# Scores tiled by 64-query blocks of both heads, with four score banks, two transfers of P and an earlier scale of V

## The chip, the cores and the metric

The kernel runs on one core of a Trainium2 chip. The metric is the device time of one execution in microseconds (us). The time before is a median of 3 runs; the profile is of one further execution.

## What is computed

Eight sequences of 576 positions go through a causal attention of 8 heads of width 64 with a window of 128 positions and a bias that falls linearly with the distance, and then through a gated MLP with a spatial mixing:

```python
scores = q @ k.T / 8 + slope[head] * -|i - j|      # only 0 <= i - j < 128, else -1e9
attn = softmax(scores);  x = attn @ v              # the heads side by side: [576, 512]
h = relu(x @ w_in);  u, v = h[:, :512], h[:, 512:]
v_n = (v - mean) / sqrt(var + 1e-6)
out = (u * (w_spatial @ v_n + b_spatial)) @ w_out
```

All of it is to float32 precision, so the kernel splits many operands into a high and a low part and multiplies three times.

## The kernel before

Sequence 0 is done by a special path (`raw_tile`), together with the splitting of the weights. Sequences 1 to 7 are done in four pairs of heads each, 28 pairs in all. What is told here is the work of one pair.

`scores` loads q and k (`qkraw`, three buffers) and v (`vraw`, three buffers). `products` multiplies q by k in blocks of 64 queries: block i has as keys the blocks i-2 to i, so 64 columns (i = 0), 128 (i = 1) or 192. One matmul is a 64x64 tile of the TensorE array: head j of the pair lies in rows 64j to 64j+63 (the array's row half), and the output goes to partitions 0 to 63 or 64 to 127 (its column half). A tile of scores before is two blocks of ONE head, even block in the lower partitions and odd block in the upper ones: 4 tiles for each head, of 128, 192, 192 and 192 columns, and a ninth of 256 columns, in which both heads' last block stand. The tiles of head 0 lie in the PSUM banks s0 and s1, those of head 1 in s2 and s3. The ninth lies in the right half of bank x0 (`plan.kept["y"]`), the bank whose left half takes the output of attention times V.

For each tile VectorE adds the bias table and takes the minimum of the negated scores (L594), ScalarE does the exponential with its sum (L599). Then, for one group of tiles at a time (j = 0: four tiles, j = 1: five), VectorE forms the reciprocals of the sums (L618, L622), ScalarE writes P's high part in fp16 to `pq` (L628), VectorE its low part (L633), and DMA transposes bring `pq` into `pt` with the keys on the partitions (L642). There is one transfer for each group and partition half: four a pair, each of 64 rows.

`attention` finds a power of two to scale V by: ScalarE takes the sum of absolute values (L654), VectorE spreads it (L661), a small DMA transpose brings it onto all partitions (L665), VectorE takes the maximum and forms the scale in five small instructions (L670 to L674), and V is split into `vh` and `vl` (L678 or L681, L685). TensorE multiplies P by V in 42 matmuls (L701) into the banks x0 and x1, and ScalarE and VectorE write the two parts of x (`xt`, L712 and L716).

`gated` runs the MLP of a sequence: V units (L768, L790) with a layer norm, u units (L820), spatial units (L841), output units (L867). The outputs are copied to `o` (L314, two buffers before) and sent off by L877.

A planner (`Plan`) sets the order of all of it. Each piece of work is added with its engine, a duration that the planner assumes and a due time; the planner plays this through and at each moment takes, of what is ready on an engine, the piece that is due first. The order that comes out is fixed at build time, and on the chip each engine keeps to it: a piece that waits holds up all that stands behind it on its engine. SyncE issues all transfers, in one order too. An attention is added only after the scores of the next pair (`AHEAD = 1`).

Of the kernel before, what the change touches and what calls it, by code (L numbers as in the profile page):

```python
# [55 lines left out]
class Plan:  # L56
# [8 lines left out]
    def __init__(self):  # L65
        self.ops, self.tags, self.kept = [], {}, {}
# [9 lines left out]
    def add(self, engine, weight, due, fn, reads=(), writes=()):  # L76
        self.either([(engine, weight, fn)], due, reads, writes)
# [22 lines left out]
    def order(self):  # L100
# [12 lines left out]
        while events or any(ready.values()):  # L113
# [8 lines left out]
            for e, heap in ready.items():  # L122
                if heap and free[e] <= now:
# [28 lines left out]
def attn_gmlp_kernel(ctx, tc, qk, v, w_in, w_spT, b_sp, w_out, outT):  # L152
# [17 lines left out]
    T0, TN = 2 * D, 3 * W  # L170
    HEAD = T0 + TN
    QSPLIT = 2 * P

# [23 lines left out]
    plan.kept["y"] = [plan.kept["x"][0][:, 2 * P:]]  # L197

# [23 lines left out]
    tabl = fixed([P, NP, 2 * P], BF16, "tabl")  # L222
# [6 lines left out]
    NT = 2 * (NQ - 1) + 1  # L229
    prob = fixed([P, 2 * HEAD + 2 * P], F32, "prob")  # L230
    PLANE = [7 * P, 9 * P]
    BASE = [0, 2 * PLANE[0] + D]
    BLOCK = [0, 14]
    PQ = BASE[1] + 2 * PLANE[1] + D
    pq = fixed([P, PQ], F16, "pq")
    stat = [fixed([P, 4, NT], F32, f"stat{i}") for i in range(2)]

# [58 lines left out]
    def tables():  # L296
        plan.add("POOL", 700, 60000, lambda: nc.gpsimd.memset(tabl(), MASKED), (), [(tabl, 0), (tabl, 1)])
        heads = [(told, h) for h in range(H)]
        for i in range(2):
            rows, cs = slice(i * D, (i + 1) * D), slice(i * D, i * D + W)  # L300

            def f(rows=rows, cs=cs):
                nc.sync.dma_start(tabs()[rows], told()[rows, :, cs])
            plan.add("SP", 800, 60000, f, heads, [(tabs, i)])

            def f(rows=rows, cs=cs, i=i):
                src = told()[rows].rearrange("p (a b) n -> p a b n", b=2)
                nc.sync.dma_start(tabl()[rows, :, (1 - i) * D:(1 - i) * D + W], src[:, :, i, cs])
            plan.add("SP", 800, 60000, f, heads, [(tabl, i)])
# [233 lines left out]
    def clear():  # L543
        plan.add("POOL", 2500, 0, lambda: nc.gpsimd.memset(pq(), 0.0), (), parts(pq, 0, PQ, 64))
# [6 lines left out]
    def pieces(p):  # L551
        out = []
        for j in range(2):
            for t in range(NQ - 1):
                n = T0 if t == 0 else W
                out.append((2 * j + (t == 3), (2 * W, 0, W, 0)[t], n, j * HEAD + (0 if t == 0 else T0 + (t - 1) * W),
                            BASE[j] + (0 if t == 0 else T0 + (t - 1) * 2 * P + D), PLANE[j], lambda h=2 * p + j, n=n: tabs()[:, h, W - n:]))
        out.append((4, 0, 2 * P, 2 * HEAD, BASE[1] + PLANE[0], PLANE[1], lambda: tabl()[:, p, :]))
        return out

    def products(p, due, st, raw, RAWS, first):
# [3 lines left out]
        flat = lambda k: sc[k]() if len(sc[k]().shape) == 2 else sc[k]().rearrange("p a b -> p (a b)")  # L565
        tiles = pieces(p)
        if first:
            def f():
                for j in range(2):
                    nc.vector.memset(flat(2 * j)[:D, 2 * W:2 * W + D], MASKED)  # L570
                nc.vector.memset(sc[4]()[:D, :D], MASKED)
                nc.vector.memset(sc[4]()[D:, W:], MASKED)
            plan.add("DVE", 400, due - 5500, f, (), [(x, 0) for x in sc])

        def f():
            def one(k, c0, j, half, i, back):
                a, z = max(0, (i - 2) * D), (i + 1) * D
                nc.tensor.matmul(flat(k)[half * D:(half + 1) * D, c0 + a - back:c0 + z - back], raw()[j * D:(j + 1) * D, 0, i * D:z],  # L578
                                 raw()[j * D:(j + 1) * D, 1, a:z], start=True, stop=True, skip_group_check=True)
            for j in range(2):  # L580
                one(4, (1 - j) * D, j, j, 2 * NQ - 2, (2 * NQ - 4) * D)
            for t in range(NQ - 1):
                for half in range(2):
                    for j in range(2):
                        i = 2 * t + half
                        one(tiles[j * (NQ - 1) + t][0], tiles[j * (NQ - 1) + t][1], j, half, i, (i - 2) * D + (D if t == 0 else 0))
        plan.add("PE", SWITCH + pe(*[4 * W] * NQ), due - 5000, f, RAWS, [(x, 0) for x in sc])
        for k, (bank, c0, n, pc, _, _, tab) in enumerate(tiles):
            pt = lambda pc=pc, n=n: prob()[:, pc:pc + n]
            t, j = (NQ - 1, 0) if k == NT - 1 else (k % (NQ - 1), k // (NQ - 1))  # L590
            d = due - 4500 + t * 700 + j * 200
# [369 lines left out]
```

## Time and profile before

| | us |
|---|---|
| median of 3 runs (lowest, highest) | 649.78 (649.24, 650.79) |
| the profiled execution, its own time | 649.93 |
| its span, first to last instruction | 648.2 |
| TensorE busy / idle in the span | 592.7 / 55.5 |
| VectorE busy | 517.1 |
| ScalarE busy | 379.8 |

The mean granted clock of TensorE is 0.983 of full speed. The 28 pairs are under way from about 75 us to 583 us of the span; ahead of that stand sequence 0 and the weights, after it the last two sequences' MLP. Busy time of TensorE is the time in which at least one matmul runs; the rest is idle, and the views of waits tell for each engine which instruction of another engine, or which transfer (DMA), ended an idle stretch.

### The profile page before, as it was taken

The numbers are of one execution on the slowest core, as the hardware profiler recorded it, in microseconds if no ns is written. First come the engines' busy times: TensorE is split into PE (matmuls) and PEld (weight loads), VectorE is DVE, ScalarE is ACT, GpSimd is POOL, SyncE is SP. The second block draws the span as 40 slices with busy tenths as digits, with TensorE's granted clock in tenths as the row PEclk, the third lists the DMA queues.
The fourth block names the chain that finished last, engine by engine and source line by source line (L and its number), as shares of the span: only waits on it lengthen the run. The fifth ranks groups of instructions, "written<-read, shape, count | busy, mean of one in ns | idle before, by whom it ended". The sixth has DMA issues, their size and how long they took to land. (4 is left out here: it accounts for less than half of the span.)

```text
span 648.2 us, 14898 instructions
## 1 busy us (share of the span) xinstructions
PE 592.7 (91%) x5392; PEld 520.3 (80%) x5392; DVE 517.1 (80%) x1913; ACT 379.8 (59%) x1200; POOL 33.2 (5%) x53
## 2 busy tenths in 40 slices
PE   4886898989899989998999989998999989899997
PEld 2444568888699879897899969897899968898997
DVE  7999989979968797887869788888968899943632
ACT  4677667767836575556646575555746586822211
POOL 2000020000100001000100001000100001000100
PEclk9997799999999999999999999999999999999999
DMA  8952217679646694378636674478647774531001
GB/s 259 335 147 78 73 43 130 154 137 192 134 78 136 133 198 76 91 162 156 119 77 123 153 189 72 87 162 161 123 87 140 138 143 70 91 80 37 2 18 56
DMA packets 147502, 78.41 MB, mean 121 GB/s; under 512 B 126818, under 2 KB 138082, under 8 KB 147428
## 3 DMA queue, kind: packets, MB, share of 16 engines
q1 hardware_dynamic: 147428, 77.46, 55.6%
q8 instruction: 42, 0.69, 0.5%
q14 instruction: 32, 0.26, 0.1%
HBM read 37.13 MB, written 9.44 MB: 72 GB/s over the span
## 5 line engine op out<-in xcount | busy, mean ns | idle before, releaser
L599 ACT ACTIVATE prob<-prob,stat 128x192 f32<-128x192 f32 (+2 forms) x252 | 109.7, 437 | 28.6 <-DVE stat L594 28.5
L841 PE MATMUL m<-wsp,vn 128*128 128x288 f32 x768 | 122.6, 298 | 3.5 <-DVE o L314 1.8
L820 PE MATMUL m<-xt,win 128*128 128x288 f32 x768 | 111.7, 298 | 6.0 <-ACT u L318 1.8
L628 ACT ACTIVATE pq<-prob,stat 128x192 f16<-128x192 f32 (+2 forms) x252 | 92.4, 439 | 37.9 <-issue 24.7
L841 PEld LDWEIGHTS m<-wsp,vn 128*128 128x128 f32 x768 | 107.5, 188 | 8.6 <-DVE o L314 3.4
L867 PE MATMUL m<-gs,wout 128*128 128x288 f32 x768 | 111.1, 299 | 2.2 <-DVE u L319 1.4
L820 PEld LDWEIGHTS m<-xt,win 128*128 128x128 f32 x768 | 103.8, 188 | 11.2 <-ACT u L318 3.8
L867 PEld LDWEIGHTS m<-gs,wout 128*128 128x128 f32 x768 | 103.8, 188 | 6.8 <-DVE u L319 1.7
L768 PE MATMUL m<-win,xt 128*128 128x512 f32 x384 | 94.3, 399 | 1.7 <-DVE vt L799 1.0
L633 DVE SCALAR_TENSOR_TENSOR pq<-prob,stat,pq 128x192 f16<-128x192 f32 (+2 forms) x252 | 90.8, 404 | 2.0 <-ACT pq L628 1.9
L768 PEld LDWEIGHTS m<-win,xt 128*128 128x128 f32 x384 | 72.2, 191 | 20.5 <-ACT pq L628 1.7
L849 DVE TENSOR_TENSOR u<-m,u 128x288 f32<-128x288 f32 x64 | 29.1, 454 | 45.5 <-PE m L841 45.2
L594 DVE CUSTOM_DVE_ANT_0 prob<-s,tabs 128x128 f32<-128x128 f32 (+1 forms) x224 | 62.9, 336 | 1.4 <-PE s L578 1.3
L738 POOL TENSOR_TENSOR st<-st,nhalf 128x1 f32<-128x1 f32 (+1 forms) x40 | 25.7, 643 | 557.2 <-DVE st L734 201.1
L578 PE MATMUL s<-qkraw 64*64 64x192 f32 (+2 forms) x896 | 50.5, 319 | 0.0
L599 ACT ACTIVATION_READ_ACCUMULATOR prob<-prob,stat 128x1 f32 x252 | 47.3, 188 | 0.0
L701 PE MATMUL x<-pt,vh 128*64 128x128 f16 (+2 forms) x784 | 43.8, 230 | 3.2 <-DMA pt<-pq 3.2
L318 ACT ACTIVATE u<-m 128x288 f32<-128x288 f32 x53 | 21.5, 405 | 40.5 <-PE m L820 40.5
L701 PEld LDWEIGHTS <-vh 128*64 128x64 f16 x784 | 35.0, 110 | 10.1 <-issue 5.5
L314 ACT COPY o<-m 128x288 f32<-128x288 f32 x28 | 11.2, 400 | 51.1 <-PE m L867 46.8
L578 PEld LDWEIGHTS s<-qkraw 64*64 64x64 f32 x896 | 39.2, 137 | 0.9
L701 PE MATMUL x<-pt,vl 128*64 128x256 f16 x392 | 35.7, 228 | 0.9 <-DVE vl L685 0.9
(139 smaller groups left out, 817.3 us busy)
## 6 DMA issues: line engine op xcount, KB each, us to landing
qkraw<-in_qk_dram SPq DMA_DIRECT2D x28, 576.0 KB, 4.5
out_dram<-o SPq DMA_DIRECT2D x64, 144.0 KB, 2.4
vraw<-in_v_dram SPq DMA_DIRECT2D x28, 320.0 KB, 3.8
vn<-in_w_in_dram SPq DMA_DIRECT2D x6, 512.0 KB, 7.9
wout<-in_w_out_dram SPq DMA_DIRECT2D x4, 512.0 KB, 7.9
pt<-pq SPq DMA_TRANSPOSE x112, 4.2
gs<-in_w_spT_dram SPq DMA_DIRECT2D x4, 288.0 KB, 5.0
xt<-in_w_in_dram SPq DMA_DIRECT2D x2, 512.0 KB, 6.6
```

The costliest lines, as they stand in the source:

```text
L578: nc.tensor.matmul(flat(k)[half * D:(half + 1) * D, c0 + a - back:c0 + z - back], raw()[j * D:(j + 1) * D, 0, i * D:z], raw()[j * D:(j + 1 ...
L594: nc.vector.tensor_tensor_reduce(pt(), flat(bank)[:, c0:c0 + n], tab(), -0.125, 3e38, ALU.add, ALU.min, st()[:, NM, k:k + 1])
L599: nc.scalar.activation(pt(), pt(), AF.Exp, bias=st()[:, NM, k:k + 1], scale=-1.0, accum_out=st()[:, SM, k:k + 1])
L628: nc.scalar.activation(pq()[:, qc:qc + n], prob()[:, pc:pc + n], AF.Copy, scale=st()[:, RC, k:k + 1])
L633: nc.vector.scalar_tensor_tensor(pq()[:, qc + plane:qc + plane + n], prob()[:, pc:pc + n], st()[:, RC, k:k + 1], pq()[:, qc:qc + n], ALU.m ...
L701: nc.tensor.matmul(xp()[j * D:(j + 1) * D, x0:x0 + w], l()[:, kt, j * D:(j + 1) * D], pts().rearrange("p a b -> p (a b)")[:, c:c + w], sta ...
L738: nc.gpsimd.tensor_tensor(st()[:m, 11:12], st()[:m, 10:11], nhalf()[:m], ALU.pow)
L768: nc.tensor.matmul(pt(), xt[c]()[:, X0[a] + t * P:X0[a] + (t + 1) * P], win()[:, c, w, DH:DF], start=(n == 0), stop=(n == 3 * NC_ - 1))
L820: nc.tensor.matmul(pt()[:, :HS], win()[:, c, w, d * P:(d + 1) * P], xt[c]()[:, X0[a] + hf * HS:X0[a] + (hf + 1) * HS], start=(n == 0), sto ...
L841: nc.tensor.matmul(pt()[:, :HS], l, r, start=(n == 0), stop=(n == len(ops) - 1))
L849: nc.vector.tensor_tensor(u(), pt()[:, :HS], u(), ALU.mult)
L867: nc.tensor.matmul(pt()[:, :HS], wout[d]()[:, w, e * P:(e + 1) * P], gs[d]()[:, a, :], start=(n == 0), stop=(n == 3 * ND - 1))
```

## The change

1. A tile of scores is one block of 64 queries of BOTH heads. Head 0 stands in the lower partitions and head 1 in the upper ones, in odd blocks the other way round. There are again nine tiles, of 64, 128 and seven times 192 columns. The bias table `tabs` follows that; the ninth tile's own table `tabl` goes, and with it the memsets of masked corners in PSUM.
2. Even blocks go to the banks s0 and s1, odd blocks to s2 and s3. No tile of scores lies in x0 any more.
3. The groups for reciprocals and transfers are the five even blocks and the four odd ones. P goes out in two transfers a pair, of 128 rows each, 18 and 14 blocks of 128 columns.
4. In P times V the columns of one matmul are picked in runs of 64 from the even and the odd part of `pt` (`queries`).
5. In the planner: the loads of q, k and v are due 4 us earlier, the scale of V 5 us earlier; a transfer of P is taken as 3 us and lands 1 us later, the small transfer of V's scale lands 1.5 us later (`lag`).
6. The output tile `o` has four buffers instead of two.

```diff
-    def add(self, engine, weight, due, fn, reads=(), writes=()):
+    def add(self, engine, weight, due, fn, reads=(), writes=(), lag=0):
+        self.late[len(self.ops)] = lag
...
+                    end += self.late.get(n, 0)
...
-    plan.kept["y"] = [plan.kept["x"][0][:, 2 * P:]]
...
-    PLANE = [7 * P, 9 * P]
-    BASE = [0, 2 * PLANE[0] + D]
+    BLOCKS = [*range(0, NB, 2), *range(1, NB, 2)]
+    EVENS = (NB + 1) // 2
+    WIDTH = [min(i + 1, 3) * D for i in BLOCKS]
+    PLANE = [2 * EVENS * P - P, 2 * (NB - EVENS) * P - P]
+    BASE = [0, 2 * PLANE[0]]
...
-    WINDOWS = (((0, (0, 256), 0), (1, (2 * P, 128), 128)),
-               ((1, (3 * P, 128), 0), (2, (4 * P, 256), 0), (3, (6 * P, 128), 128), (3, (0, None), 256), (4, (P, None), 256)))
+    WINDOWS = (((0, 4, 0, 0), (1, 2, 0, 128)),
+               ((1, 2, 1, 0), (2, 4, 0, 0), (3, 2, 0, 128), (3, 1, 1, 256), (4, 1, 0, 256)))
+    def places(k):
+        i = BLOCKS[k]
+        bank, c0 = ((0, 3 * P), (2, 3 * P), (0, 0), (2, 0), (0, W), (2, W), (1, 0), (3, 0), (1, W))[i]
+        odd = i % 2
+        return i, odd, bank, c0, sum(WIDTH[:k]), BASE[odd] + (0 if i < 2 else P + (i // 2 - 1) * 2 * P + odd * D), WIDTH[k]
+    def queries(pts, j, a, kt, n, s):
+        x = [BASE[o] + a * PLANE[o] + 2 * kt * P + s * P + (j ^ o) * D for o in range(2)]
+        flat = pts().rearrange("p a b -> p (a b)")
+        if n == 1:
+            return flat[:, x[0]:x[0] + D]
+        ap = flat[:, x[0]:x[0] + D]
+        steps = [[x[1] - x[0], 2], [1, D]]
+        return bass.AP(ap.tensor, ap.offset, [ap.ap[0], [P, 2], *steps] if n == 4 else [ap.ap[0], *steps])
...
-        sc = [plan.buf(ps, "s", 4, [P, 512], F32) for _ in range(4)] + [plan.buf(ps, "y", 1, [P, 2 * P], F32)]
+        sc = [plan.buf(ps, "s", 4, [P, 512], F32) for _ in range(4)]
...
+            order = sorted(range(NB), key=lambda k: (BLOCKS[k] // 2, BLOCKS[k]))
+            for k in order:
+                i, odd, bank, c0, _, _, n = places(k)
                 for j in range(2):
+                    rows = slice((j ^ odd) * D, ((j ^ odd) + 1) * D)
+                    nc.tensor.matmul(flat(bank)[rows, c0:c0 + n], raw()[j * D:(j + 1) * D, 0, i * D:(i + 1) * D],
+                                     raw()[j * D:(j + 1) * D, 1, (i + 1) * D - n:(i + 1) * D], start=True, stop=True, skip_group_check=True)
...
-            d = due - 4500 + t * 700 + j * 200
+            d = due - 4500 + k * 350
...
-        raw, vr = load(b, p, [due - 12000], [NQ])
+        raw, vr = load(b, p, [due - 16000], [NQ])
...
-            ks = range(NQ - 1) if j == 0 else range(NQ - 1, NT)
+            ks = range(EVENS) if j == 0 else range(EVENS, NB)
...
-            for half in range(2):
-                c0 = BASE[j] + (1 - half) * D
-                def f(j=j, half=half, nb=nb, c0=c0):
-                    rows = slice(half * D, (half + 1) * D)
-                    nc.sync.dma_start_transpose(out=pts()[:, BLOCK[j]:BLOCK[j] + nb, rows], in_=pq()[rows, c0:c0 + nb * P])
-                plan.add("SP", 1700, d + 1500 + half, f, parts(pq, c0, c0 + nb * P, 64), [(pts, (j, half))])
+            c0, n = BASE[j], 2 * PLANE[j]
+            def f(c0=c0, n=n):
+                nc.sync.dma_start_transpose(out=pts()[:, c0 // P:(c0 + n) // P, :], in_=pq()[:, c0:c0 + n])
+            plan.add("SP", 3000, d + 1500, f, parts(pq, c0, c0 + n, 64), [(pts, j)], lag=1000)
...
-        d = due - 3000
+        d = due - 8000
...
-        plan.add("SP", 300, d + 2, f, [(vl, 0)], [(vl, 1)])
+        plan.add("SP", 300, d + 2, f, [(vl, 0)], [(vl, 1)], lag=1500)
...
-            o = plan.buf(work, "o", 2, [P, HS], F32)
+            o = plan.buf(work, "o", 4, [P, HS], F32)
```

## Rows read from the trace of the kernel before

**Rows 1.** Page, part 1: busy us, share of the span, instructions.
```profile
PE 592.7 (91%) x5392; PEld 520.3 (80%) x5392; DVE 517.1 (80%) x1913; ACT 379.8 (59%) x1200; POOL 33.2 (5%) x53
```

**Rows 2.** Windows, two sequences: stretch, length, busy by engine, clock, DMA share, GB/s.
```profile
304.40:378.50 74.10, 70.15 (x674) 63.54 (x674) 60.01 (x228) 44.14 (x145) 3.33 (x5) 0.98 0.60 126
378.50:450.70 72.20, 68.45 (x672) 62.40 (x672) 59.94 (x227) 44.17 (x145) 3.33 (x5) 1.00 0.64 129
```

**Rows 3.** Waits of PE: who for whom, us in total, times, longest.
```profile
PE x L578 <- DVE xt L716: 11.8, 5, 3.1
...
PE x L701 <- DMA pt<-pq: 3.2, 5, 1.4
...
PE x L578 <- DVE x L572: 2.1, 1, 2.1
PE m L841 <- DVE o L314: 1.8, 3, 0.9
```

**Rows 4.** Timeline of PE at one sequence's end: start, length, what, [idle before].
```profile
372.07 0.41 PE L701 MATMUL x<-pt,vh 128*64 128x256 f16 x4
...
373.54 1.89 PE L867 MATMUL m<-gs,wout 128*128 128x288 f32 x12
378.49 0.38 PE L578 MATMUL x<-qkraw 64*64 64x192 f32 x2 [3.06 <-DVE xt L716]
...
380.15 3.02 PE L768 MATMUL m<-win,xt 128*128 128x512 f32 x12
```

**Rows 5.** Timeline of ACT in the same stretch.
```profile
373.67 1.44 ACT L628 ACTIVATE pq<-prob,stat 128x128 f16<-128x128 f32 x4 [2.53 <-issue]
377.14 0.40 ACT L314 COPY o<-m 128x288 f32<-128x288 f32 x1 [2.02 <-DMA out_dram<-o]
377.44 0.90 ACT L712 ACTIVATE xt<-x,am 128x256 fp32r<-128x256 f32 x2
```

**Rows 6.** Timeline of DVE in the same stretch.
```profile
371.80 0.29 DVE L670 TENSOR_REDUCE am<-vl 128x1 f32<-128x128 bf16 x1 [0.75 <-DMA vl<-vl]
...
373.42 0.17 DVE L622 RECIPROCAL stat<-stat 128x4 f32<-128x4 f32 x1
...
377.95 0.97 DVE L716 SCALAR_TENSOR_TENSOR xt<-x,am,xt 128x256 fp32r<-128x256 f32 x2 [2.20 <-ACT xt L712]
```

**Rows 7.** Waits of all engines: two of DVE for transfers.
```profile
DVE am L670 <- DMA vl<-vl: 16.3, 14, 2.1
...
DVE o L314 <- DMA out_dram<-o: 8.5, 5, 2.6
```

**Rows 8.** Windows, 2 us behind the wait that ended at 304.4 us.
```profile
306.00:308.00 2.00, 2.00 (x12) 1.22 (x5) 2.00 (x12) 1.49 (x7) 0.00 (x0) 0.50 0.88 135
```

**Rows 9.** Source view of L578, 378 to 381 us: ns least/median/most.
```profile
L578 PE MATMUL s<-qkraw x32: 216/322/373, 378.5 to 379.9; 64*64 64x192 f32 x24, 64*64 64x64 f32 x4, 64*64 64x128 f32 x4
...
L578 PE MATMUL x<-qkraw x4: 322/348/373, 378.5 to 378.7; 64*64 64x192 f32 x4
```

**Rows 10.** Groups by form, DVE L594: count | busy us, mean ns | idle.
```profile
L594 DVE CUSTOM_DVE_ANT_0 prob<-s,tabs 128x192 f32<-128x192 f32 x168 | 50.7, 353 | 0.1
...
L594 DVE CUSTOM_DVE_ANT_0 prob<-s,tabs 128x128 f32<-128x128 f32 x56 | 14.2, 287 | 1.3 <-PE s L578 1.3
...
L594 DVE CUSTOM_DVE_ANT_0 prob<-x,tabl 128x256 f32<-128x256 f32 x28 | 11.7, 419 | 0.5 <-PE x L530 0.3 <-ACT xt L712 0.2
```

**Rows 11.** Tile view of pt, SyncE's issue of P's transfers: ns least/median/most.
```profile
L642 SPq DMA_TRANSPOSE pt<-pq x112: 1234/1640/4089, 95.4 to 570.6; - x112
```

**Rows 12.** Source view of L665, SyncE's issue of the small transfer.
```profile
L665 SPq DMA_TRANSPOSE vl<-vl x28: 1112/1516/2532, 120.8 to 560.7; - x28
```

**Rows 13.** DMA issues: count, median us from issue to landing.
```profile
pt<-pq SPq DMA_TRANSPOSE x112, 4.2
```

**Rows 14.** Timeline of DVE ahead of the first pair's scores.
```profile
73.05 0.34 DVE L490 CUSTOM_DVE_ANT_0 pt<-s,pt 64x192 f32<-64x192 f32 x1
```

More of the change, by code (lines that the diff above doesn't have):

```diff
@@ L65, in __init__ @@
     def __init__(self):
-        self.ops, self.tags, self.kept = [], {}, {}
+        self.ops, self.tags, self.kept, self.late = [], {}, {}, {}
     def buf(self, pool, tag, bufs, shape, dtype):
@@ L221, in attn_gmlp_kernel @@
     tabs = fixed([P, H, W], BF16, "tabs")
-    tabl = fixed([P, NP, 2 * P], BF16, "tabl")
     win = fixed([P, NC_, 2, DF], F32R, "win")
@@ L228, in attn_gmlp_kernel @@
     l2 = fixed([P, DH], F32R, "l2")
-    NT = 2 * (NQ - 1) + 1
-    prob = fixed([P, 2 * HEAD + 2 * P], F32, "prob")
-    PLANE = [7 * P, 9 * P]
-    BASE = [0, 2 * PLANE[0] + D]
[L233 to L236, printed above, removed]
+    BLOCKS = [*range(0, NB, 2), *range(1, NB, 2)]
+    EVENS = (NB + 1) // 2
+    WIDTH = [min(i + 1, 3) * D for i in BLOCKS]
+    prob = fixed([P, sum(WIDTH)], F32, "prob")
+    PLANE = [2 * EVENS * P - P, 2 * (NB - EVENS) * P - P]
+    BASE = [0, 2 * PLANE[0]]
+    pq = fixed([P, 2 * sum(PLANE)], F16, "pq")
+    stat = [fixed([P, 4, NB], F32, f"stat{i}") for i in range(2)]
     rstat = fixed([P, 8, 8], F32, "rstat")
@@ L296, in tables, with f @@
     def tables():
-        plan.add("POOL", 700, 60000, lambda: nc.gpsimd.memset(tabl(), MASKED), (), [(tabl, 0), (tabl, 1)])
         heads = [(told, h) for h in range(H)]
         for i in range(2):
-            rows, cs = slice(i * D, (i + 1) * D), slice(i * D, i * D + W)
-            def f(rows=rows, cs=cs):
-                nc.sync.dma_start(tabs()[rows], told()[rows, :, cs])
+            def f(i=i):
+                if i == 0:
+                    nc.sync.dma_start(tabs()[:D], told()[:D, :, :W])
+                    return
+                dst, src = (x.rearrange("p (a b) n -> p a b n", b=2) for x in (tabs()[D:], told()[D:, :, D:D + W]))
+                for j in range(2):
+                    nc.sync.dma_start(dst[:, :, j], src[:, :, 1 - j])
             plan.add("SP", 800, 60000, f, heads, [(tabs, i)])
[L306 to L309, printed above, removed]
     def copy(n, ap, due, reads, writes, fast=False):
@@ new lines, in clear @@
+        plan.add("POOL", 2500, 0, lambda: nc.gpsimd.memset(pq(), 0.0), (), parts(pq, 0, 2 * sum(PLANE), 64))
+    WINDOWS = (((0, 4, 0, 0), (1, 2, 0, 128)),
[5 more added lines that the diff above has]
+        return i, odd, bank, c0, sum(WIDTH[:k]), BASE[odd] + (0 if i < 2 else P + (i // 2 - 1) * 2 * P + odd * D), WIDTH[k]
@@ L587, in products, with f @@
         plan.add("PE", SWITCH + pe(*[4 * W] * NQ), due - 5000, f, RAWS, [(x, 0) for x in sc])
-        for k, (bank, c0, n, pc, _, _, tab) in enumerate(tiles):
+        for k in range(NB):
+            i, odd, bank, c0, pc, _, n = places(k)
             pt = lambda pc=pc, n=n: prob()[:, pc:pc + n]
-            t, j = (NQ - 1, 0) if k == NT - 1 else (k % (NQ - 1), k // (NQ - 1))
-            d = due - 4500 + t * 700 + j * 200
-            def f(bank=bank, c0=c0, n=n, pt=pt, tab=tab, k=k):
-                nc.vector.tensor_tensor_reduce(pt(), flat(bank)[:, c0:c0 + n], tab(), -0.125, 3e38, ALU.add, ALU.min, st()[:, NM, k:k + 1])
+            d = due - 4500 + k * 350
+            def f(bank=bank, c0=c0, n=n, pt=pt, odd=odd, k=k):
+                nc.vector.tensor_tensor_reduce(pt(), flat(bank)[:, c0:c0 + n], tabs()[:, 2 * p + odd, W - n:], -0.125, 3e38, ALU.add, ALU.min,
+                                               st()[:, NM, k:k + 1])
@@ L595, in products @@
             cols = parts(prob, pc, pc + n, 64)
-            plan.add("DVE", dve(n), d, f, [(sc[bank], 0)] + [(x, i) for x in (tabs, tabl) for i in range(2)], cols + [(st, (NM, k))])
+            plan.add("DVE", dve(n), d, f, [(sc[bank], 0)] + [(tabs, i) for i in range(2)], cols + [(st, (NM, k))])
             def f(pt=pt, k=k):
```

70 lines of the change are left out of this document (17 added, 53 removed).

## The prediction

> **What bounds the kernel now.** I read the page's busy times first, then windows of whole sequences, then the waits, then one sequence's end in the timeline. TensorE is busy 91% of the span and VectorE 80% [rows 1], so a gain must come out of the 55.5 us in which TensorE idles. In a settled sequence (from one late score group to the next) TensorE is busy for 68 to 70 us of 72 to 74, VectorE for 60 [rows 2]: VectorE has 12 us of slack in each, and TensorE's stream sets the pace. So the edits are worth what they take out of TensorE's idle time, and VectorE and ScalarE count only where TensorE waits for them.
>
> The reader is to see in the waits that the largest one behind the start-up is one pattern: the score matmuls L578 wait 11.8 us, five times, for VectorE's L716 [rows 3]. L716 writes x, and has nothing to do with scores. They meet because the ninth score tile lies in bank x0. The timeline shows the chain once whole. P times V ran from 372.07 to 373.5 us, then an output unit; the next score group began only at 378.49, after 3.06 us of idling, and V units followed at 380.15 [rows 4]. It waited for L716, which waited 2.20 us for ScalarE's L712. L712 stood behind four L628 and a copy to `o`. The L628 started at 373.67, when VectorE had done the reciprocal L622 at 373.42, itself queued behind L670, which waited 0.75 us for the transfer of V's scale. The copy waited another 2.02 us for an older output to be sent off [rows 5, 6]. Three edits hit this chain: bank, V's scale, four `o` buffers.
>
> **The change part by part.** The sum is made against the profiled execution, 649.93 us (span 648.2, 1.7 around it); the median of the runs is 0.15 us below it, so the two are one.
>
> *Score tiles out of x0.* With the bank alone, a score group could start right behind the output unit. Group and switch take 1.66 us (378.49 to 380.15, [rows 4]), and then the V units need x, which L716 delivers where it does now. So of a wait w about min(w, 1.6) is saved: 5 x 1.6 = 8.1 us. The other 3.7 us come only if L716 is earlier too. Its delay was, in the chain above, 2.02 us of `o` and 0.75 us of V's scale; both are attacked, and over the run VectorE waits 16.3 us for V's scale and 8.5 us for `o` [rows 7]. I take 11.8, bounds 8.1 and 11.8.
>
> *The clock.* Behind the wait that ended at 304.4 us the granted clock was 0.50 [rows 8], the lower of its two levels (1.2 GHz), though behind the 3.06 us wait at 378 it stayed at 1.00 [rows 2]. The sequence with the dip has 70.15 us of busy TensorE against 68.45 in the next, at 674 and 672 matmuls [rows 2]: 1.7 us. It goes with the idling ahead of it. I take 1.7, bounds 0 and 1.7.
>
> *Transfers of P.* Four of 64 rows become two of 128, of the same bytes. No row shows a 128-row one of this size. Issue: a transfer of 14 or 18 blocks takes SyncE 1.23 us at least, 1.64 at the median when it follows another [rows 11]; the small one, a single block of 128 rows, already takes 1.11 [rows 12]. So issue is nearly a fixed price, and two issues a pair go: 2 x 1.23 to 2 x 1.64 us of SyncE's time, off the path. Landing: a group's second half is issued some 1.64 us after the first and lands 4.2 us later [rows 13], 5.8 us in all. The single transfer is bounded by 4.2 (as one half, saves 1.6) and, if twice the rows take twice the 4.2, by 8.4 (loses 2.6); as issue is mostly fixed I take 5.0, 0.8 us earlier. P times V waits for it 3.2 us in five places, 0.64 on average [rows 3]. I take 2.0 of the 3.2, bounds 3.2 gained and 5 x 2.6 = 13 lost.
>
> *Output buffers.* TensorE waits 1.8 us for VectorE's copies to `o` [rows 3], part of which is behind the 8.5 us that these wait for the sending [rows 7]. I take half, 0.9; bounds 0 and 1.8.
>
> *First pair.* Its score group waits 2.1 us for the memset L572 [rows 3], which goes. Next it would wait for VectorE to have read the bank for sequence 0: L490 began at 73.05 us and took 0.34 [rows 14], so 73.4 in place of the 74.8 at which the wait ended. I take 1.4, bounds 0 and 2.1.
>
> *Widths.* Of nine tiles, one of 128 and one of 256 columns become one of 192 and one of 64. VectorE's L594 takes 353, 287 and 419 ns at 192, 128 and 256 [rows 10]; 66 ns for 64 columns make the narrow one some 221, an estimate. So 287 + 419 - 353 - 221 = 132 ns a pair, twice that with L633 over the same columns: 28 x 0.26 = 7.4 us of VectorE's time, and a like amount on ScalarE. It is covered by TensorE (60 of 72 us), so I take 0; the bounds are 0 and, if VectorE were the pace, 7.4.
>
> *Matmuls.* Scores stay 18 matmuls of the same widths; only the order over the four quarters of the array changes, and each four still fall on four quarters. P times V stays 42 matmuls, but the moving operand comes in runs of 64 columns. No row shows a stepped one. Bounds: 0, or as long again as the whole group, 372.07 to 373.54 or 1.47 us a pair [rows 4], 41 us in all. The columns read stay the same in number, so I take 0.
>
> *V's scale and loads.* The same instructions, earlier. L654, L661, the transfer L665 and L670 to L685 pass the L628 and L633 of their pair and the transfers of P on SyncE. The planner now allows 1.5 us more to land, so L670 should stand where its transfer is in, and L622 and L633 behind it no longer wait. What is queued behind a late one is now the previous pair's work. If v isn't there, L654 holds ScalarE with L599 behind it; the load is moved by 4 us against 5, so 1 us of slack goes, at most 28 us of a ScalarE that is idle for 268 [rows 1]. I take 0 beyond the 3.7 us above. `tabl`'s memset and two transfers (against one more for `tabs`) lie early in the start-up, under the weights: 0.
>
> *New waits.* The planner's whole order is made anew from other durations, and the trace can't price that. I allow 0.9 us lost, the size of the smallest term; bounds 4 gained and 5 lost.
>
> Sum: 11.8 + 1.7 + 2.0 + 0.9 + 1.4 - 0.9 = 16.9, and 649.93 - 16.9 = 633.0 us. With the low ends of the positive terms (8.1, no clock, no transfer, no buffer, no first pair) and the 5 lost, 646.8; with the high ends (11.8, 1.7, 3.2, 1.8, 2.1, 4) 625.3. The 13, 41 and 7.4 belong to other cases.
>
> **The rivals.** *The wait only moves.* Scores start early, but x is no earlier: V units wait in place of the scores. For it speaks that ScalarE still has the L628 ahead of L712; against it, that V's scale leaves the chain. It gives 8.1 from the bank and 1.4 from the first pair: 640.4 us, with others' bounds 637 to 645.
>
> *The two heads collide in their bank.* After the change, the matmuls of both heads of one block, from the two row halves of the array, write the same bank at the same time, on different partitions; before, only the ninth tile did. Place: each score group. Price: if every such pair had to run one after the other, a group of 1.66 us would take twice that, 28 x 1.66 = 46 us, and 633 + 46 = 679. It decides from 16.9 / 28 = 0.6 us a group on: beyond that the kernel is slower than before. Against it stands the ninth tile: its four matmuls have 322 to 373 ns each, and the first two, one in each half, take 0.38 us together [rows 4, 9]. All 36 of a group, 322 ns at the median, fit in 1.66 us. So they overlap, also in one bank. I give it 0.03.
> The Trainium skill, TensorEngine Tiling (Array Packing), section Restrictions and Gotchas, says that different row tiles cannot access the same PSUM bank simultaneously. By that rule the sum would be this rival's; this case's trace disagrees for tiles on different partitions, at 0.38 us for two.
>
> *Operand or transfer is slow.* The runs of 64 columns, or the 128-row transfers, come out near their upper bounds: 633 + 41 = 674, or 633 + 2 + 13 = 648 at the five places. The latter would be no change. Nothing in the trace speaks for either.
>
> *No change.* Another order of the planner eats all. It would need 17 us of new waits, more than the largest wait that TensorE has now (11.8, [rows 3]).
>
> **How the numbers follow.** Forecast 0.68; the wait only moves 0.20; collision 0.03; slow operand 0.03; no change by transfers or order 0.03; slower by the new order, some 655, 0.03. The likeliest's time is 633.0, its own range 626 to 640. The range 624 to 645 takes in the second case and leaves out about 0.15. A measurement of this kernel can tell a change of about 0.2%, 1.3 us. Faster: 0.68 + 0.20 = 0.88; same 0.03; slower 0.09.
>
> **What would show it.** Right: no wait of L578 for L716, and no matmul of L578 that writes x; TensorE's idle time down to about 40 us; L670's wait for its transfer from 16.3 to under 5 us; the waits for `o` nearly gone; TensorE's busy time lower only by the clock; score groups still 1.66 us. Two transfers a pair, landing near 5 us. Wrong: waits of L768 for xt at each sequence's end of 1 us or more (the first rival), a score group near 3 us (the second), P times V well over 1.47 us (the third), or L701 waiting for the transfer at more than five places.

## The result and the profile after

The changed kernel takes 617.07 us (median of four runs, 616.75 to 617.54), beside it the kernel before 649.51: a ratio of 0.950, 95% interval 0.948 to 0.952. The gain is 32.4 us; 16.9 were forecast, and the range ended at 624. The profiled execution took 617.34 us, its span is 615.4. Against the span of before that is 32.8 us less, of which TensorE's idle time gave 17.6 (55.5 to 37.9) and its busy time 15.2 (592.7 to 577.5). The forecast put 15.2 us into the first and 1.7 into the second: it had the first nearly right and the second nearly not at all. (Of e14 below, two of ten executions were disturbed, at 802.9 and 3119.61 us where the others took 642 to 647; they are left out, and as one of them is the profiled one, its profile is not read.)

Busy times of the page, kernel after; beside [rows 1], TensorE's share rose from 91% to 94%:

```profile
PE 577.5 (94%) x5392; PEld 513.2 (83%) x5392; DVE 508.7 (83%) x1902; ACT 379.3 (62%) x1207; POOL 31.7 (5%) x52
```

Windows of the first pair (72 to 95 us) and of two settled sequences, kernel after (length, then busy time and instructions of each engine, granted clock, DMA share, GB/s):

```profile
72.00:95.00 23.00, 17.63 (x144) 12.56 (x144) 22.76 (x70) 12.15 (x44) 4.70 (x3) 1.00 0.30 65
240.40:308.40 68.00, 66.97 (x672) 61.80 (x672) 58.67 (x226) 44.43 (x146) 3.26 (x5) 1.00 0.61 137
308.40:376.42 68.02, 66.99 (x673) 61.82 (x673) 58.75 (x226) 44.48 (x146) 3.26 (x5) 1.00 0.59 137
```

A settled sequence takes 68.0 us where it took 72 to 74 [rows 2], and one idle microsecond is left in it. TensorE's own work in it has fallen too, to 67.0 us from 68.45 and 70.15. At the first pair the clock is full; before, it was not.

The first stretch again, and the part of it at half clock, kernel before:

```profile
72.00:95.00 23.00, 20.31 (x144) 14.19 (x144) 20.04 (x72) 14.80 (x54) 4.45 (x3) 0.78 0.21 73
...
73.50:83.70 10.20, 8.84 (x71) 5.90 (x75) 7.72 (x37) 6.36 (x28) 0.00 (x0) 0.50 0.19 61
```

For 10.2 us the granted clock stood at 0.50, the lower of its two levels (1.2 GHz); the same 144 matmuls of the 23 us kept TensorE busy for 20.31 us there and for 17.63 after. The prediction had read only the 3.4 us dip at 305 us [rows 8].

TensorE's longest wait in the kernel after (waiting line and releaser: us in total, times, longest):

```profile
PE m L801 <- ACT u L313: 5.9, 7, 1.0
```

and a row of ScalarE, which was 4.4 us before:

```profile
ACT vh L667 <- DVE am L660: 14.9, 14, 2.1
```

The 11.8 us of score matmuls waiting for x, the 3.2 us for P's transfer and the 2.1 us for the memset [rows 3] are gone. So are VectorE's 16.3 us for V's scale and 8.5 us for `o` [rows 7]: no row of VectorE names a transfer. What TensorE waits for in each settled sequence is up to one microsecond at a u unit (L801), for a bank that ScalarE reads; before, ScalarE cost the u units 1.8 us in all. ScalarE now waits longer for V's scale, off the path (e13 below).

TensorE's timeline, kernel after, one late pair:

```profile
264.40 1.64 PE L574 MATMUL s<-qkraw 64*64 64x64 f32 x36
265.97 1.85 PE L848 MATMUL m<-gs,wout 128*128 128x288 f32 x12
267.74 0.41 PE L683 MATMUL x<-pt,vh 128*64 128x256 f16 x4
...
269.21 3.08 PE L848 MATMUL m<-gs,wout 128*128 128x288 f32 x21
```

The score group takes 1.57 us from its start to the next unit's, where it took 1.66 [rows 4]. P times V takes 267.74 to 269.21, 1.47 us, as before [rows 4]: the operand in runs of 64 columns costs nothing. Both heads write one bank in every group, and the group is no longer for it; the rule of the Trainium skill, TensorEngine Tiling (Array Packing), section Restrictions and Gotchas, that different row tiles cannot use one bank at a time, is not borne out here for tiles on different partitions, now in 28 groups of 18 matmuls (36 in the trace, which has two records for each).

SyncE's issues of P's transfers, kernel after (ns least/median/most):

```profile
L628 SPq DMA_TRANSPOSE pt<-pq x56: 1541/2680/3892, 92.2 to 548.7; - x56
```

They land 4.7 us behind their issue at the median, near the 5.0 forecast. Added up over the trace, the issues took 193.8 us of SyncE before and 129.0 after. With all other transfers SyncE spent 321 us on issuing before (58% of the time in the stretch of the pairs, 75 to 583 us) and 241 after. What that did to the small transfer of V's scale can be read from the trace: before, SyncE issued it on average 3.1 us behind the VectorE instruction that it waits for (L661), and for 2.9 us of these SyncE was issuing other transfers. After, it is 1.4 us and 1.2.

### The profile page after: what moved, and what is told of

It is laid out like the page before. It is cut to its first block, busy times and chain, and to the rows that moved or that the text cites. A ratio compares the mean times of both kernels' runs of the same rounds, so it can differ in the third digit from the quotient of the medians.

```text
span 615.4 us, 14769 instructions
## 1 busy us (share of the span) xinstructions
PE 577.5 (94%) x5392; PEld 513.2 (83%) x5392; DVE 508.7 (83%) x1902; ACT 379.3 (62%) x1207; POOL 31.7 (5%) x52
## 4 chain that ended last, share of the span: by engine, by line
PE 64%; DVE 27%; ACT 5%; issue 2%; DMA 1%; SPq 0%; POOL 0%; ACTq 0%; POOLq 0%
PE m L822 18%; PE m L848 16%; PE m L801 12%; PE m L749 5%; PE x L683 5%; PE s L574 4%; DVE st L710 3%; DVE pq L622 2%; PE m L771 2%; DVE vt L723 2%; DVE prob L583 2%; DVE vn L760 1%; ACT prob L589 1%; DVE vl L671 1%; DVE prob L485 1%
## 5 line engine op out<-in xcount | busy, mean ns | idle before, releaser
L589 ACT ACTIVATE prob<-prob,stat 128x192 f32<-128x192 f32 (+2 forms) x252 | 107.0, 427 | 36.4 <-DVE stat L583 36.3
L822 PE MATMUL m<-wsp,vn 128*128 128x288 f32 x768 | 120.2, 297 | 0.0
L801 PE MATMUL m<-xt,win 128*128 128x288 f32 x768 | 110.0, 297 | 9.2 <-ACT u L313 5.9
L801 PEld LDWEIGHTS m<-xt,win 128*128 128x128 f32 x768 | 103.8, 188 | 13.2 <-ACT u L313 7.7
L617 ACT ACTIVATE pq<-prob,stat 128x192 f16<-128x192 f32 (+2 forms) x252 | 88.4, 427 | 4.6 <-issue 1.3
L622 DVE SCALAR_TENSOR_TENSOR pq<-prob,stat,pq 128x192 f16<-128x192 f32 (+2 forms) x252 | 88.6, 389 | 2.1 <-ACT pq L617 1.5
L583 DVE CUSTOM_DVE_ANT_0 prob<-s,tabs 128x192 f32<-128x192 f32 (+2 forms) x252 | 70.2, 329 | 7.4 <-PE s L574 7.4
L574 PE MATMUL s<-qkraw 64*64 64x192 f32 (+2 forms) x1008 | 46.1, 311 | 0.5 <-DVE stat L583 0.5
L574 PEld LDWEIGHTS s<-qkraw 64*64 64x64 f32 x1008 | 35.6, 133 | 5.2 <-issue 3.4
L683 PEld LDWEIGHTS <-vh 128*64 128x64 f16 x784 | 33.1, 110 | 6.5 <-issue 5.5
L313 ACT ACTIVATE vt<-m 128x512 f32<-128x512 f32 x31 | 18.5, 596 | 29.2 <-DVE st L714 17.7
L710 DVE BATCH_NORM_STATS2 st<-vt 128x6 f32<-128x512 f32 (+1 forms) x40 | 27.5, 687 | 10.3 <-ACT vt L313 10.3
```

The source lines that it names most:

```text
L574: nc.tensor.matmul(flat(bank)[rows, c0:c0 + n], raw()[j * D:(j + 1) * D, 0, i * D:(i + 1) * D], raw()[j * D:(j + 1) * D, 1, (i + 1) * D - ...
L583: nc.vector.tensor_tensor_reduce(pt(), flat(bank)[:, c0:c0 + n], tabs()[:, 2 * p + odd, W - n:], -0.125, 3e38, ALU.add, ALU.min, st()[:, N ...
L589: nc.scalar.activation(pt(), pt(), AF.Exp, bias=st()[:, NM, k:k + 1], scale=-1.0, accum_out=st()[:, SM, k:k + 1])
L617: nc.scalar.activation(pq()[:, qc:qc + n], prob()[:, pc:pc + n], AF.Copy, scale=st()[:, RC, k:k + 1])
L622: nc.vector.scalar_tensor_tensor(pq()[:, qc + PLANE[j]:qc + PLANE[j] + n], prob()[:, pc:pc + n], st()[:, RC, k:k + 1], pq()[:, qc:qc + n], ...
L683: nc.tensor.matmul(xp()[j * D:(j + 1) * D, x0:x0 + n * D], l()[:, kt, j * D:(j + 1) * D], queries(pts, j, a, kt, n, s), start=j not in see ...
```

## The experiments

All ratios are against the kernel before, run beside; an interval is 95%. Kernels are the kernel after with one edit where nothing else is said.

**Parts of the change.** e2 is the kernel before with the planner's part alone, e3 the kernel after without it and with two output buffers, e4 and e5 take back one of these each. In e3 the transfers of P also lose the 1 us by which the planner lets them land later.

```diff
# e2: on the kernel before; e3: the reverse of it on the kernel after
-        raw, vr = load(b, p, [due - 12000], [NQ])
+        raw, vr = load(b, p, [due - 16000], [NQ])
-        d = due - 3000
+        d = due - 8000
-        plan.add("SP", 300, d + 2, f, [(vl, 0)], [(vl, 1)])
+        plan.add("SP", 300, d + 2, f, [(vl, 0)], [(vl, 1)], lag=1500)
# e4 (and e3): on the kernel after; e5: the three edits above taken back
-            o = plan.buf(work, "o", 4, [P, HS], F32)
+            o = plan.buf(work, "o", 2, [P, HS], F32)
```

> The kernel before with the planner's part alone: loads of q, k and v due 4 us earlier, V's scale due 5 us earlier, its small transfer taken to land 1.5 us later. Theory W (the gain is waits that go, each with its tail): VectorE's 16.3 us of waiting for V's scale falls under 5, and the score groups' 11.8 us wait for x shrinks by up to 3.7, since the scale stands in its chain; 643 to 647 us. Rival L (the gain comes with the new layout of the scores: free bank, balanced quarters of the array, the clock of the first pair): the scale's wait goes but the time stays at 648 to 651.

> The changed kernel with its planner's part and its output buffers put back: V's scale and loads due as before, no extra landing times, two buffers for o. So the new score tiles, banks and two transfers alone. Rival L: nearly all of the gain is here, 618 to 623 us, with score groups of 1.31 us. Theory W: x0's wait goes (8 us), the score groups shrink (3 us) and the first pair's low clock may go (5 us), but the waits for V's scale and for the outputs' sending stay: 628 to 636.

> The changed kernel with two buffers for o in place of four. Theory W: VectorE and ScalarE wait some 10 us again for outputs to be sent, and TensorE's units wait for them in turn, part of it too briefly to show as idle: 619 to 623 us. Rival L: nothing on the path, 616.5 to 618.

> The changed kernel with V's scale and the loads due as before and without the extra landing time of the small transfer. Theory W: VectorE waits about 16 us for V's scale again, P's reciprocals and x stand behind it, and the V units of each sequence start later: 621 to 627 us. Rival L: 616.5 to 619.

| | us | ratio | interval |
|---|---|---|---|
| e2 planner's part alone | 637.84 | 0.980 | 0.976 to 0.983 |
| e3 all but the planner's part, two `o` | 619.19 | 0.951 | 0.948 to 0.953 |
| e4 two `o` | 616.70 | 0.948 | 0.945 to 0.951 |
| e5 old V scale and loads | 617.82 | 0.949 | 0.946 to 0.951 |

e3, e4 and e5 came out as their rival L had it; e2 was faster than both of its theories. The planner's part alone is worth 13 us, and nothing once the rest of the change is there. The output buffers are worth nothing in the kernel after. So terms of the change don't add: two of them cure one thing.

The wait of the score groups for x, 11.8 us before [rows 3], is in e2:

```profile
PE x L580 <- DVE xt L718: 1.8, 2, 1.1
```

It went with the ninth tile still in x0. VectorE's wait for V's scale fell from 16.3 us to 3.7. SyncE's queue is as crowded in e2 as before (197 us for P's issues, the small transfer still 2.6 us behind its source): the scale is only asked for early enough. Which of the part's three numbers does this was not tested.

**Four transfers again, and more issues without more of P's data.** e6 sends each transfer of P as two of 64 rows. e10 leaves P's transfers alone and puts a small one behind each that nobody reads.

```diff
# e6
-                nc.sync.dma_start_transpose(out=pts()[:, c0 // P:(c0 + n) // P, :], in_=pq()[:, c0:c0 + n])
+                for rows in (slice(0, D), slice(D, P)):
+                    nc.sync.dma_start_transpose(out=pts()[:, c0 // P:(c0 + n) // P, rows], in_=pq()[rows, c0:c0 + n])
# e10, with four scratch tiles and two output buffers
+                nc.sync.dma_start_transpose(out=spare[turn[0] % 4](), in_=tabs()[:, 0, :P])
```

> The changed kernel with each of the two transfers of P issued as two, of 64 partitions each, back to back; all else, the planner's order too, as in the changed kernel. If one transfer of 128 rows lands earlier than two of 64 (my term of 2.0 us), P times V waits again in some places and SyncE is held 2.5 to 3.3 us more a pair: 619 to 621 us. Rival: the landing is set by the bytes and the order has slack, 616.5 to 618.

> The kernel after with two output buffers and, behind each transfer of P, one further transpose of a single block of 128 by 128 bf16 values into a scratch tile that nobody reads: as many issues on SyncE as with four transfers a pair, but P itself still goes out in one piece. Theory S (the 11 us of the four transfers are SyncE's issue time, about 1.1 to 1.7 us for each further one, which makes V's scale and the loads late): about 626 to 630 us, and VectorE waits for the small transfer again. Theory D (they come from the 64-row transfers themselves, of which the second lands later): 617 to 619 us.

e6 took 628.26 us, 0.966 (0.964 to 0.969), more than both theories gave it. e10 took 637.25 us, 0.980 (0.976 to 0.984), well above theory S's 626 to 630; theory D falls. The issue rows, first of e6, then of e10's extra transfers:

```profile
L629 SPq DMA_TRANSPOSE pt<-pq x112: 1240/1716/2705, 92.0 to 562.0; - x112
```

```profile
L630 SPq DMA_TRANSPOSE spare<-tabs x56: 1217/1236/2254, 95.5 to 571.0; - x56
```

and VectorE's waits for V's scale, in e6 and in e10:

```profile
DVE am L657 <- DMA vl<-vl: 12.3, 14, 2.6
```

```profile
DVE am L659 <- DMA vl<-vl: 15.5, 15, 2.6
```

The wait that the change had removed is back in both, though the small transfer itself lands within 2.3 to 2.5 us. What is late is its issue: SyncE does one after the other, and in e6 and e10 the small transfer is issued 3.0 and 3.4 us behind its source again, 2.8 and 3.1 of them spent on other transfers. P's issues add up to 194.0 us in e6 (129.0 in the kernel after), in e10 to 135.4 and the extra ones to 83.1. So 65 us more of SyncE cost 10.6 us of time (the difference of the ratios times 649.5), and 90 us more cost 19.4 (20.8 against e4, which has e10's two output buffers). V's scale isn't all that is late in e10: VectorE and ScalarE wait 15.4 us for the sending of outputs, where it is 1.2 in e4.

**Outputs off SyncE's queue.** e15 is the kernel before, e16 the kernel after, with one word changed.

```diff
-                nc.sync.dma_start(outT[e * P:(e + 1) * P, b, hf * HS:(hf + 1) * HS], o())
+                nc.gpsimd.dma_start(outT[e * P:(e + 1) * P, b, hf * HS:(hf + 1) * HS], o())
```

> The kernel before with one edit: the 64 outputs are sent off by GpSimd's queue in place of SyncE's, so that SyncE has 29.8 us less to issue and no transfer stands behind an output that isn't ready. Theory N: V's scale and the loads come earlier, the wait of VectorE for the small transfer falls from 16.3 to under 10 us, and the time to 638 to 645 us. If SyncE's queue isn't what holds the kernel up: 648 to 651 us. If issuing delays the layer norm's piece on GpSimd: above 651 us.

> The kernel after with its 64 outputs sent off by GpSimd's queue: SyncE has 24.5 us less to issue. In the kernel after no engine waits for the small transfer any more, so SyncE's queue should be worth little there: 614 to 617.5 us. If its queue still costs as much as in the runs with more issues (11.2 us for 65 us of issuing, 0.17 us each): 612 to 614 us. If issuing delays the layer norm's piece on GpSimd: 618 to 625 us.

e15 took 642.28 us, 0.989 (0.984 to 0.993), as theory N had it, though VectorE's wait for V's scale fell to 12.8 us only, and not under 10. What fell more are VectorE's wait for `o`, from 8.5 us [rows 7] to 1.1, and the score groups' wait for x, from 11.8 us [rows 3] to:

```profile
PE x L578 <- DVE xt L716: 2.9, 4, 1.1
```

e16 took 621.57 us, 0.956 (0.951 to 0.962): some 4 us slower than the kernel after, inside what its expectation gave for a delayed layer norm; but that is not the cause. A settled sequence of e16, and its end behind the last matmul:

```profile
240.40:308.40 68.00, 66.99 (x672) 61.82 (x672) 58.69 (x226) 44.50 (x147) 7.61 (x13) 1.00 0.61 137
612.40:619.80 7.40, 0.01 (x1) 0.00 (x0) 0.00 (x0) 0.40 (x1) 0.54 (x1) 0.63 0.11 40
```

and the end of the kernel after and of e15:

```profile
612.10:615.40 3.30, 0.00 (x0) 0.00 (x0) 0.00 (x0) 0.40 (x1) 0.00 (x0) 1.00 0.18 60
```

```profile
633.10:640.50 7.40, 0.02 (x1) 0.00 (x0) 0.00 (x0) 0.40 (x1) 0.54 (x1) 0.68 0.11 40
```

e16's sequences are those of the kernel after to 0.02 us, and its last matmul ends 0.3 us later. The loss is in the 7.4 us behind that matmul, where the kernel after has 3.3; the same tail is in e15. It isn't the last output itself, which lands 2.8 us behind the last matmul (2.3 in the kernel after). The program's end waits for a drain of GpSimd, here in e16 (ns least/median/most):

```profile
L938 POOLq DRAIN  x3: 40/102/5862, 613.2 to 619.5; - x3
```

It takes 5.86 us, in the kernel after at most 0.69. Measured by the last matmul's end in the profiled executions, e15 gains 644.8 - 633.1 = 11.7 us, and e16 nothing; by the ratio e15 gains 7.5 us, with 3.1 either way, its longer tail included. So what SyncE's queue cost by the outputs in the kernel before, it no longer costs. The Trainium skill, Trainium Kernel Development and Optimization, section Key Constraints, says that transfers issued from several engines run on the same DMA engines, so that spreading them saves only the sequencer's issue time; these two runs fit that, and show what thinning the queue can be worth: 11.7 us where it is crowded, nothing where it is not. The 11.7 us are not issue time alone: no transfer stands behind an output that isn't ready any more, and the two were not separated.

**The last tile in x0.** e9 puts the last block's tile back, from sequence 2 on (`late`; bank 4 is the right half of x0; the first four pairs stay as they are after); e12 is e9 and e6 together; e14 is e12 without the planner's part and with two `o`, so that against the kernel before little but the tiles differs.

```diff
+    plan.kept["y"] = [plan.kept["x"][0][:, 2 * P:]]
...
+                if late and i == 8:
+                    bank, c0 = 4, 0
```

> The changed kernel with the last block's tile of scores, both heads, in the right half of bank x0 from sequence 2 on, as the ninth tile was before; the other eight tiles as in the changed kernel. Theory W: score groups wait again for VectorE's L697 (x), about 1.5 to 2 us at each of five or six sequence ends: 624 to 629 us. Rival (the wait for x only stood there because V's scale and the outputs were late): 617 to 620.

> The kernel after with four transfers of P and with the last block's tile in x0 from sequence 2 on: both edits, which cost 11.2 and 7.5 us alone. If the two add, 635 to 637 us. If they share a cause (both make V's scale and x late, so that one wait covers the other), 628 to 632 us. If each makes the other's wait longer, as the prediction's chain through x0, the output and V's scale would have it, over 639 us.

> The tiles alone: the kernel after with four transfers of P, the last block's tile in x0 from sequence 2 on, two output buffers, and the old due times without extra lags. Against the kernel before only the tiles differ (one block of both heads; even and odd banks; widths; the order over the quarters of the array; the stepped operand). Theory N (the planner's part and the fewer transfers are two cures for one thing, SyncE's crowded queue, and without both it is back): what is left is the quarters' balance, 3.0 us, and the narrower tiles on VectorE and ScalarE, about 3.5 us as the added copy cost: 641 to 646 us. Theory T (the tiles themselves are worth the 17 us that four transfers and x0 together left): 631 to 637 us.

e9: 624.56 us, 0.961 (0.958 to 0.963). The time is in theory W's range, but not by its mechanism: no score group waits for x. The u units wait longer for ScalarE, 9.6 us in place of 5.9, and ScalarE's L699, which writes x, waits for score matmuls in x0, as it doesn't in the kernel after:

```profile
PE m L807 <- ACT u L315: 9.6, 7, 1.8
...
ACT xt L699 <- PE x L578: 4.5, 5, 1.2
```

Against the kernel after, 3.5 us of TensorE's idle time and 3.3 of its busy time come in, the latter at a mean clock of 0.985 in place of 0.994. That the second wait causes the first is likely, but not shown.

e12: 633.21 us, 0.974 (0.970 to 0.978), between "add" and "share a cause"; by ratios the loss is 15.8 us against 17.7 for the two alone, and the interval (some 3 us either way) holds the sum. e14: 645.29 us, 0.992 (0.989 to 0.995), theory N; theory T falls. With that the change can be walked in steps:

| step | from, to | gain, us |
|---|---|---|
| tiles alone | before, e14 | 5.2 ± 1.9 |
| planner's part, four `o` | e14, e12 | 11.6 ± 3.3 |
| two transfers for four | e12, e9 | 8.7 ± 3.2 |
| last tile out of x0 | e9, after | 7.1 ± 2.0 |

Each gain is a difference of two ratios times 649.5 us, with the two intervals' half widths added in quadrature. In another order the middle two would trade: the planner's part was worth nothing when it came last (e3, e5). e12 still has 13.6 us of VectorE waiting for V's scale, so the 11.6 us of the planner's part can hardly be that wait; by which waits they come stays open.

**The quarters of the array.** e7 doesn't swap the heads of odd blocks, so that only two of the four quarters are used.

```diff
-                    rows = slice((j ^ odd) * D, ((j ^ odd) + 1) * D)
+                    rows = slice(j * D, (j + 1) * D)
```

> The changed kernel with the score matmuls of odd blocks written like those of even blocks: head 0 always to the lower partitions, head 1 always to the upper ones. (The scores of odd blocks so land under the other head's bias and value; the work is the same in size.) Only two of the four quarters of the array are then used. Theory Q (a group's time is the columns of its fullest quarter at four passes and 2.4 GHz): 1472 columns in place of 832 give 2.45 us in place of 1.39, 28 x 1.06 = 30 us: 645 to 648 if it all shows. Rival (the group got shorter by its order or its banks): the group stays near 1.31 us and the time near 617.

It took 638.14 us, 0.981 (0.978 to 0.983). TensorE's timeline, e7, the same late pair:

```profile
268.20 2.83 PE L574 MATMUL s<-qkraw 64*64 64x64 f32 x36
```

A group takes 1.19 us more than the 1.64 after. A quarter works through its own matmuls one after the other, and the fullest sets the time. In one quarter the records of 192 columns start 163 ns apart, and each matmul has two: 326 ns a matmul, 1.70 ns a column. From 832 columns to 1536 (the 1472 of the expectation are a miscount) that is 1.20 us. Counted in the code, the fullest quarter had 896 columns before (head 1's odd blocks and its last one) and has 832 now: 64 x 1.70 ns = 0.109 us a group, where the timelines gave 0.09, and 3.0 us over 28. Of e7's 33 us of longer groups (28 x 1.19) some 20 reached the time; most of the rest went into idling that was there anyway, for TensorE idles 26.6 us in e7 in place of 37.9.

**VectorE's narrower tiles.** e11, with two output buffers, adds one copy a pair:

```diff
+                if k == 2:
+                    nc.vector.tensor_copy(spare(), pt())
```

> The kernel after with two output buffers and one further VectorE copy of 128x192 float32 values for each pair, into a scratch tile that nobody reads, behind the third tile's minimum: some 0.25 to 0.3 us a pair, 7 to 8 us over 28 pairs, about what the wider tiles had cost before. Theory of the prediction (VectorE's time is covered by TensorE): 616.5 to 618 us. Rival (part of it is on the path, since the exponentials and the scale of V stand behind it): 619 to 625 us.

It took 620.34 us, 0.953 (0.950 to 0.956): 3.4 us above e4, its own base, with an uncertainty of 2.8. The added group (busy us, mean ns | idle before):

```profile
L587 DVE COPY spare<-prob 128x192 f32<-128x192 f32 x28 | 7.3, 260 | 1.0
```

So by the middle value about half of what VectorE does more is paid, though VectorE has 9 us of slack in each sequence. The uncertainty is nearly as large as the loss, and TensorE's mean clock was lower in e11's executions (0.988 to 0.991) than in e4's (0.992 to 0.994); so how much is paid, and how much of it through the clock, is not shown. The same two groups over the tiles, minimum and low part of P, in the kernel after:

```profile
L622 DVE SCALAR_TENSOR_TENSOR pq<-prob,stat,pq 128x192 f16<-128x192 f32 (+2 forms) x252 | 88.6, 389 | 2.1 <-ACT pq L617 1.5
L583 DVE CUSTOM_DVE_ANT_0 prob<-s,tabs 128x192 f32<-128x192 f32 (+2 forms) x252 | 70.2, 329 | 7.4 <-PE s L574 7.4
```

Together 158.8 us. Before it was 165.4 (L633's 90.8, L594's 62.9 and 11.7): 6.6 less, of the 7.4 forecast.

**The first pair, and ScalarE's wait.** e8 puts four memsets ahead of the first pair's scores again; e13 lets the planner take V's scale as done 0.8 us later.

```diff
# e8, first pair only
+                    nc.vector.memset(flat(k)[:D, 448:512], MASKED)
# e13
-        plan.add("DVE", 600, d + 4, f, [(vl, 0), (vl, 1), (powers, 0)], [(am, 1)])
+        plan.add("DVE", 600, d + 4, f, [(vl, 0), (vl, 1), (powers, 0)], [(am, 1)], lag=800)
```

> The changed kernel with four small memsets of VectorE into unused columns of the score banks put back ahead of the first pair's scores, as the kernel before had them. Theory C (the wait of the first score group for the memsets brings TensorE down to its lower clock, as in the kernel before from 73 to 84 us): the first group waits about 2 us, the granted clock falls to 0.5 behind it for some 10 us: 622 to 625 us. Rival (the dip had other causes, such as the order of the work around it): 617 to 619, clock at 1.

> The kernel after with one number changed in the planner: the five instructions of V's scale on VectorE are taken to be done 0.8 us later, so that ScalarE is given other work ahead of the high part of V, for which it waits 14.9 us in 14 places now. If that idle time of ScalarE is what delays the u units' banks (TensorE waits 1.03 us a sequence for ScalarE there), 612 to 616 us. If it is off the path, 616.5 to 618 us; another order of the planner may also make it slower, 618 to 622 us.

e8: 616.60 us, 0.948 (0.945 to 0.950). The first score group waited only about 0.5 us for the memset, and the clock did not fall there; so this is no test of what the 2.1 us wait of before cost, and the link from that wait to the 10.2 us at half clock stays open. e13: 616.90 us, 0.948 (0.945 to 0.950): ScalarE's wait for V's scale fell from 14.9 us to 1.8 and the time stayed, so that wait is off the path. No version tried is faster than the kernel after by more than the intervals.

## Why the prediction was wrong, step by step

**"A gain must come out of the 55.5 us in which TensorE idles."** This step failed, and with it "each four still fall on four quarters" and "TensorE's busy time lower only by the clock". Busy time fell by 15.2 us where 1.7 was forecast; that is nearly all that the sum missed. Three things are in it, taken from the two profiled executions. The quarters' balance, 3.0 us by e7's price. The clock: the mean granted clock rose from 0.983 to 0.994, so the time at half clock, twice what the mean lacks to 1 times the span, fell from some 22 us to some 7; matmul time under it fell from 15.4 to 4.8 us in the trace, which gives back half the difference, 5.3 us, where the prediction took 1.7. And stalls too short for a gap: a matmul's modelled end covers a late start of the next by up to about 0.2 us. In the V, u, spatial and output units at full clock, starts that came later than the unit's usual spacing, beyond any gap shown, add up to 15.4 us in 135 places before and 9.0 in 81 after, 6.4 less. Together 14.7 of the 15.2. Some four fifths of the stalled time before, and nearly three quarters after, end right behind a signal of VectorE or ScalarE. So these are in the main waits for other engines, counted as work: the busy share hid part of what could be gained.

**"Two issues a pair go ... off the path."** The amount was nearly right (65 us of SyncE; 28 times the forecast's pair is 69 to 92), the verdict wrong. SyncE was not full, but V's scale, loads and outputs stood behind P's issues, V's scale for 2.9 us on average, and TensorE waited for what came of it. The term for the transfers, 2.0 us by their landing, measured 8.7 to 10.6. TensorE's own wait for P is 2.8 us of that (e6), about what the term priced; the rest came through the queue (e10: more issues without more of P cost more still; e15: 11.7 us from the outputs off the queue).

**V's scale "0 beyond the 3.7".** In the kernel before the planner's part alone is worth 13 us (e2), because it asks for V's scale early enough for that queue; with two transfers it is worth nothing (e3, e5). The prediction saw that bank, V's scale and `o` meet in one chain, but not that SyncE's queue stands behind it, which other edits thin too, nor how much that queue costs. It had a row of it in hand: 16.3 us of VectorE waiting for the small transfer [rows 7], of which it credited 0.75 us a chain, and only where TensorE was seen to wait behind it.

**Score tiles out of x0, 11.8.** The wait of [rows 3] went, but it did not need the bank: it fell from 11.8 us to 1.8 by the planner's part (e2) and to 2.9 by taking the outputs off SyncE's queue (e15), with the tile in x0 both times. The bank was where the queue's delay showed, and the term credits it with what other edits cure as well. As the last step, without the first four pairs, the bank is worth 7.1 us, by other waits (e9); that this is near the term's lower bound of 8.1 is luck. (5 x 1.6 is 8.0.) The bank alone on the kernel before was not tried.

**Widths, 0.** Mis-sized: 6.6 us of VectorE less, worth some 3 by e11. The tiles alone, 5.2 us (e14), agree with 3.0 and 3.4 within their uncertainty; that split is argued from the prices, not measured edit by edit.

**Output buffers, 0.9, and new waits, -0.9.** The buffers measured nothing in the kernel after (e4); alone on the kernel before they were not tried. The new waits are there: the u units' for ScalarE grew from 1.8 us to 5.9.

**First pair, 1.4.** The wait for the memset went; what it was worth, with the clock behind it, was not measured (e8).

**Right:** idle time near 40 us (with luck in it, as its largest term goes by other parts of the change too, and the new waits are larger than allowed); no score matmul waits for x; landing near 5 us; a stepped operand at no cost; no collision of the heads; the waits for V's scale and `o` gone. Of the rivals, "the wait only moves" didn't come; the truth lay on the far side of the forecast, where the prediction had no case at all.

## What to carry to other kernels

Look at each queue as at an engine, SyncE's above all, and not at its share alone: SyncE issued for only 58% of the stretch of the pairs here and still held up what was wanted at once. Where an engine waits for a small transfer that lands as fast as ever, compare the transfer's issue with the end of the instruction that it depends on; if other issues fill the time between, the wait is one for the queue. Every edit that thins the queue, or that asks earlier, cures the same wait, so such gains must not be added. On tiles of the TensorE array, count the columns of the fullest quarter, not the matmuls. And do not take busy TensorE for a floor: look at the clock row over the whole span and at the spacing of starts before saying that only idle time can be won.

## What the runs showed of the hardware

A transpose's issue on SyncE has a high fixed price: 1.11 us at least for a single block of 128 rows ([rows 12]; 1.22 in e10), 1.24 for 14 or 18 blocks of 64 rows, 1.54 for as many of 128 rows. Twice the data in one issue costs 0.3 us more at the least, in a second issue 1.24; the medians are further apart, 1.72 us (e6) and 2.68 (kernel after). An output issued by GpSimd takes that engine 0.55 us (35.0 us over 64 in e16). With outputs on GpSimd's queue, the drain of GpSimd at the program's end took 5.86 us in e15 and in e16, against at most 0.69 in the kernel after.
